# Blocks 2 and 3 of a fused attention and feed-forward kernel: h for both blocks first, y by seven products, preparation jobs and opening reordered

## The chip, the cores and the metric

The kernel runs on one core of a Trainium2 chip. The metric is the time of one execution in microseconds (us), as the device reports it; three executions are shown, and their median counts.

## What is computed

Chunked attention (chunks of 32 queries, 8 memory keys, 16 keys to the left, 8 to the right), then two feed-forward layers over 3072 tokens (model width 512, inner width 2048), all in float32:

```python
scores = scale * np.matmul(q_c, k_full.transpose(0, 1, 3, 2))
a = np.exp(scores - np.max(scores, axis=-1, keepdims=True))
a = a / (np.sum(a, axis=-1, keepdims=True) + 1e-09)
out[:, :, c_start:c_end] = np.matmul(a, v_full)
...
h = x @ w_in                                              # layer 1
g = np.maximum(h, 0.0) + np.log1p(np.exp(-np.abs(h)))
y = g @ w_out
...
h = y @ w_in2                                             # layer 2
g = h - np.tanh(h)
out = g @ w_out2
```

## The kernel before

**Numbers in halves.** A float32 operand is kept as a high part (a float32r copy, made by ScalarE, ACT) and a low part (the rest, a subtraction on VectorE, DVE). `mm3` makes one product of two such operands by three matmuls on TensorE (PE): high x high, high x low, low x high. The weights come as 64-bit numbers, whose words are put together by integer work on ACT and DVE (`split_w` in the opening, `job_w` later).

**Blocks.** Tokens are worked in six blocks of 512, an attention unit being 128 tokens (24 units). Layer 1 gives y from h through g: `ff_h` makes one of 16 rows of h (12 matmuls with 512 columns), softplus gives g, `split_g` its halves `gh`, `gl`, and `ff_y1` adds that row's part to the four banks of y (12 matmuls). Block 0 runs in the opening, whose order of work stands written out by hand as tokens (`OPENING`); blocks 1, 2 and 3 alternate h and y row by row (the loop over `j` with `PLAIN`), with h in two PSUM banks (`ps_h`) and y in the four `ps_y`. Blocks 4 and 5 make all of h first (`steps`, 32 of them, h in six banks in turn) and then y for both blocks at once by seven products instead of eight (`y_phase`), as in Strassen's scheme: 7 products x 8 rows x 2 halves of the width x 3 matmuls. Layer 2 (three blocks of 1024 tokens, `PHASES`) uses seven products for h and for y. `y_steps` makes the operands of these products: per product and row a cast `gh` on ACT, a subtraction `gl` on DVE, in some steps a sum on DVE. The first three (`AHEAD`) are made ahead, and the pool `g` has three buffers for each, so the operand for row k+3 waits until PE is through with row k.

**Order of the work.** The order on every engine is the program's (a manual schedule). Behind every 12 matmuls of h, and every 12 of y, the program calls `tick()`, whose counter places everything else: attention units 8 to 23 one after the other, each starting six ticks behind the last (`ATT_STEP`, `ATT_ORDER`), and the preparation jobs at the ticks in `JOBS`: eight `job_w1` (sums of layer 1's output weights for the seven products), sixteen `job_w` (layer 2's weights: loaded at once, worked on from the fourth tick on, written back to HBM as seven operands), six `job_x` (layer 2's seven inputs for a block of 1024 tokens, made from y of layer 1). In a unit, tick 0 issues on PE the attention output of the unit before (`v_mm`) and this unit's scores (`s_mm`), and on DVE the maximum and a subtraction; tick 1 the exponential on ACT; tick 2 the sum and division on DVE; tick 4 the transposes on PE (`t_mm`). Softplus and the exponential need different tables on ACT, so a table load (`ACT_TABLE_LOAD`) stands in front of each change. Transfers are all issued from SyncE's queue (SP), in the program's order. `Ring` loads the weights of the seven products ahead, through five slots of 1 MB.

**Places that the change touches.** `OPENING` (tokens: Z zero products that PE runs to fill time, S scores, T transposes, V attention output, H and Y rows of layer 1, `l` the low part of a weight, K the storing of layer 1's weights for later; `ON_POOL` puts the named low parts on GpSimd, POOL), `VIA_DRAM` (units 20 to 22 come early in the order and go through HBM), `job_w`, `job_x`, `Ring`, `h_phase`, `y_phase`, `tick` and the main loops.

Of the kernel before, what the change touches and what calls it, by code (L numbers as in the profile page):

```python
# [22 lines left out]
P = 128  # L23
# [11 lines left out]
N = 512  # L35
# [27 lines left out]
ON_POOL = ('li0', 'l15')  # L63
# [12 lines left out]
PLAIN = NB - 2  # L76
# [4 lines left out]
GSLOT = (8, 9, 10, 11, 12, 13, 14, 7)  # L81
JOBS = (
    (1, 15, 24, 43, 53, 76, 85, 94),
    (5, 14, 23, 33, 66, 75, 84, 92, 95, 99, 102, 106, 109, 113, 117, 152),
    (42, 54, 159, 169, 214, 224),
)
SECOND = (95, 102, 109, 117)
PHASES = ((1, NT - 1),) + tuple((2, b) for b in range(NT))
# [8 lines left out]
def attention_ffn_ffn(  # L97
# [38 lines left out]
    x1d = dpool.tile([P, KT, 2, N], F32, name="x1d")  # L136
# [927 lines left out]
```

## Time and profile before

| what | value |
|---|---|
| median of three executions | 1057.54 us (1057.13 to 1058.17) |
| the profiled execution | 1057.51 us |
| its span, first to last instruction | 1055.4 us |
| mean granted clock of TensorE, share of full | 0.997 |
| busy in the span: PE, DVE, ACT, POOL | 1044.2, 727.6, 567.1, 7.8 us |
| moved by DMA | 303.19 MB, mean 287 GB/s |

The span is what the rows of the trace cover; the profiled execution is 2.1 us longer, for what lies around it. A busy time is the sum of an engine's instructions. Matmuls are pipelined and their ends are modelled, so PE's pace is read from the starts of its rows rather than from its busy time. In the lists of instructions each row has a start, a duration, engine, line and operation, and in brackets the engine's idle time before it with the work that ended it.

### The profile page before, as it was taken

Reading aid. Unit: us, or ns where it says so; the run is one execution under the profiler, and the core shown is the slowest. Engines: PE = TensorE matmul, PEld = TensorE weight load, DVE = VectorE, ACT = ScalarE, POOL = GpSimd, SP = SyncE. Lnnn points to the kernel's source line nnn. Section 1 sums busy time; section 2 is a strip of 40 time slices with the busy share of each in tenths; the row PEclk is TensorE's granted clock in tenths of the full one; section 3 lists DMA queues with packets and bytes.
Section 4 is the critical chain, followed back from the end, with each engine's and each line's share of the span. In section 5 each row is a group of like instructions: output and inputs, shape, how many; then the busy total and the mean of one; then the engine's idle time right before and its main releaser. Section 6 shows DMA issues by size and latency. Waiting matters only on the chain.

```text
span 1055.4 us, 18458 instructions
## 1 busy us (share of the span) xinstructions
PE 1044.2 (99%) x7368; PEld 857.4 (81%) x7370; DVE 727.6 (69%) x1129; ACT 567.1 (54%) x904; POOL 7.8 (1%) x14
## 2 busy tenths in 40 slices
PE   7999999999999999999999999999999999999998
PEld 5787888888888888888888888888888888888886
DVE  6998445845755657487677687777487877446876
ACT  6996454645656455354454555544455554344553
POOL 2000000000000000000000000000000000000000
PEclk8999999999999999999999999999999999999999
DMA  9989945857777986999987999978799788656651
GB/s 377 407 327 358 337 171 186 301 187 236 263 248 248 312 307 195 341 361 352 325 326 281 359 371 347 341 294 320 272 363 347 293 321 305 224 170 213 243 202 61
DMA packets 101269, 303.19 MB, mean 287 GB/s; under 512 B 8000, under 2 KB 55104, under 8 KB 83520
## 3 DMA queue, kind: packets, MB, share of 16 engines
q1 hardware_dynamic: 101184, 302.02, 79.5%
q8 instruction: 58, 0.95, 0.4%
q14 instruction: 27, 0.22, 0.1%
HBM read 211.29 MB, written 90.70 MB: 286 GB/s over the span
## 4 chain that ended last, share of the span: by engine, by line
PE 97%; DVE 1%; ACT 1%; DMA 0%; issue 0%; ACTq 0%
PE ps_y L387 47%; PE ps_h L387 32%; PE ps_b L387 13%; PE ps_a L361 2%; PE ps_a L280 1%; PE ps_a L332 1%; PE ps_h L880 1%; DMA qk<-in_qk 0%; PE ps_yy L361 0%; PE ps_h L399 0%; DVE gl L427 0%; DVE t L307 0%; DVE x L327 0%; ACT o L170 0%; PE ps_a L268 0%
## 5 line engine op out<-in xcount | busy, mean ns | idle before, releaser
L387 PE MATMUL ps_h<-x,w 128*128 128x512 f32 x900 | 215.3, 390 | 0.1
L704 ACT CAST gh<-w 128x512 fp32r<-128x512 f32 x224 | 139.0, 622 | 140.3 <-DVE gl L645 120.2
L645 DVE TENSOR_TENSOR gl<-w,gh 128x512 fp32r<-128x512 f32 x236 | 163.0, 691 | 71.4 <-ACT gh L704 64.9
L387 PEld LDWEIGHTS ps_h<-x,w 128*128 128x128 f32 x900 | 168.6, 188 | 35.4 <-ACT t L410 0.2
L387 PE MATMUL ps_y<-gh,w 128*128 128x512 f32 x512 | 172.9, 399 | 0.0
L387 PEld LDWEIGHTS ps_y<-gh,w 128*128 128x128 f32 x512 | 96.1, 188 | 21.3
L387 PE MATMUL ps_y<-gh,x 128*128 128x512 f32 x352 | 109.4, 389 | 0.0
L387 PE MATMUL ps_y<-gl,w 128*128 128x512 f32 x256 | 99.7, 390 | 0.0
L387 PE MATMUL ps_y<-w,x 128*128 128x512 f32 x402 | 94.5, 389 | 0.0
L387 PEld LDWEIGHTS ps_y<-w,x 128*128 128x128 f32 x402 | 75.5, 188 | 15.7
L427 DVE TENSOR_TENSOR gl<-t,gh 128x512 fp32r<-128x512 f32 x64 | 45.5, 713 | 55.8 <-ACT gh L422 55.6
L668 ACT ACTIVATE tanh<-sum 128x512 f32<-128x512 f32 x72 | 45.5, 632 | 60.0 <-DVE sum L641 59.8
L387 PEld LDWEIGHTS ps_y<-gh,x 128*128 128x128 f32 x352 | 66.1, 188 | 13.7
L410 ACT ACTIVATE t<-ps_h 128x512 f32<-128x512 f32 x64 | 38.1, 598 | 69.4 <-PE ps_h L387 65.8
L387 PE MATMUL ps_b<-gh,x 128*128 128x512 f32 x176 | 68.5, 389 | 0.0
L387 PE MATMUL ps_h<-gh,x 128*128 128x512 f32 x176 | 68.5, 389 | 0.0
L387 PE MATMUL ps_y<-gl,x 128*128 128x512 f32 x176 | 68.5, 389 | 0.0
L448 ACT CAST o<-c 128x1024 fp32r<-128x1024 f32 (+1 forms) x32 | 31.0, 969 | 69.6 <-DVE c L493 41.1
L645 DVE TENSOR_TENSOR w<-w 128x512 f32<-128x512 f32 x88 | 60.5, 688 | 6.8 <-ACT w L410 5.8
L387 PEld LDWEIGHTS ps_y<-gl,w 128*128 128x128 f32 x256 | 48.2, 188 | 9.0
L387 PE MATMUL ps_y<-x,w 128*128 128x512 f32 x240 | 55.2, 389 | 0.0
L387 PE MATMUL ps_b<-w,x 128*128 128x512 f32 x216 | 54.8, 389 | 0.0
(160 smaller groups left out, 1611.6 us busy)
## 6 DMA issues: line engine op xcount, KB each, us to landing
x<-wod SPq DMA_DIRECT2D x44, 1024.0 KB, 4.7
w<-x2d SPq DMA_DIRECT2D x21, 1024.0 KB, 6.8
x<-wid SPq DMA_DIRECT2D x21, 1024.0 KB, 6.1
wod<-o SPq DMA_DIRECT2D x32, 512.0 KB, 6.1
qk<-in_qk SPq DMA_DIRECT2D x21, 768.0 KB, 6.5
x2d<-o SPq DMA_DIRECT2D x30, 512.0 KB, 7.2
x<-wid SPq DMA_DIRECT2D x18, 768.0 KB, 6.8
ring<-wod SPq DMA_DIRECT2D x12, 1024.0 KB, 5.3
```

Of the source, the lines that this page charges most:

```text
L280: nc.tensor.matmul(out=ps[cc, j, KEYS * p : KEYS * (p + 1)], lhsT=a["q"][r, p, cc], rhs=a["k"][r, c, p, :], start=True, stop=True,)
L332: nc.tensor.transpose(ps[:, p * P : (p + 1) * P], a["sm"][:, p * P : (p + 1) * P], ident)
L361: nc.tensor.matmul(out=ps[h : h + 64, p % 2, 2 * P + t0 : 2 * P + t0 + CHUNK], lhsT=v, rhs=pT, start=True, stop=True,)
L387: nc.tensor.matmul(out=ps, lhsT=a, rhs=b, start=first and i == 0, stop=last and i == 2, skip_group_check=on,)
L410: nc.scalar.activation(out=out, in_=x, func=AF.Softplus)
L427: eng.tensor_tensor(out=gl, in0=t, in1=gh.bitcast(F32), op=ALU.subtract)
L448: nc.scalar.copy(out=hi, in_=src)
L645: nc.vector.tensor_tensor(out=out, in0=x, in1=y, op=ALU.subtract)
L668: nc.scalar.activation(out=t, in_=h, func=AF.Tanh)
L704: nc.scalar.copy(out=gh, in_=src)
L880: nc.tensor.matmul(out=ps_h[1], lhsT=zeros[:, :P], rhs=zeros, start=True, stop=True)
```

## The change

1. **Blocks 2 and 3** are worked as blocks 4 and 5 are: 32 steps of h (block 2 with rows 0 to 15, then block 3 with rows 15 to 0), then y of both by seven products (`y_phase(0)`), with y in the four banks `ps_y` and weights from a ring in slots `w0` to `w4`. Only block 1 still alternates. `PHASES` gets a first phase, the loads of layer 1's weights get ticks of their own (`T1_LOADS`), and the ring for the later phases is made apart.
2. **Attention** goes in plain order, at ticks written out (`ATT_AT`); units 20 to 22 no longer go through HBM. Units 10, 11, 21 and 22 (`LATE_ACT`) get the form of softmax that the opening uses for some units: eight small exponentials on ACT that also add up, in place of one wide one with a subtraction and a sum on DVE. Units with four ticks have their transposes at tick 3 in place of 4. Units 20 to 23 now lie beside `y_phase(0)`.
3. **Jobs** get other ticks. Nine of the sixteen `job_w` (`BY_ACT`) put their words together with two more passes on ACT and two fewer on DVE. Two of the sums become one. The jobs that work between ticks 105 and 121 split in two pieces, with tiles of the pool `g` (`split_halves`).
4. **Opening**: zero products in more and smaller groups (8, 4, 1, 2, 3, 7, 2 in place of 7, 8, 11), some tokens in another order, one low part (`li0`) on DVE in place of POOL, `K` tokens elsewhere.

```diff
-ATT_STEP = 6
-ATT_ORDER = (8, 9, 10, 11, 20, 12, 13, 14, 15, 21, 16, 17, 18, 19, 22, 23)
-VIA_DRAM = (20, 21, 22)
+ATT_AT = (0, 6, 14, 20, 28, 33, 38, 42, 46, 50, 54, 59, 64, 68, 74, 86, 92)
...
-Z7 S0 mx0 qa1 qb1 ex0 Z8 S1 ml0 qa2 qb2 T0 mx1 qa3 S2 pT0 qb3 ex1 S3 mx2 mx3 ex2 V0 ml1 ex3 ml2 T1
-yi0 ml3 T2 xh0 pT1 xl0 T3 pT2 si0 V1 yo0 pT3 xh1 V3 so0 hi0 y1 li0 V2 xh3 xl1 xh2 xl3 y2 s1 xl2 Z11
-H0 h1 s2 ho0 S4 l1 h2 y3 H1 l2 K1 c10 s3 y4 H2 c30 lo0 h3 c40 c11 l3 Y0 c31 y5 s4 H3 c41 h4 s5 c12
+Z8 S0 mx0 qa1 qb1 ex0 Z4 S1 qa2 ml0 qb2 qa3 Z1 T0 mx1 S2 pT0 qb3 ex1 S3 mx2 mx3 ex2 Z2 V0 ml1 ex3
+ml2 T1 yi0 ml3 Z3 T2 xh0 pT1 xl0 T3 pT2 si0 V1 yo0 pT3 V3 xh1 so0 hi0 y1 xl1 V2 xh3 li0 xl3 xh2 s1
+y2 xl2 Z7 H0 h1 s2 S4 ho0 l1 h2 y3 Z2 H1 l2 K1 c10 s3 y4 H2 c30 lo0 h3 c40 c11 l3 Y0 c31 y5 s4 H3
...
-ON_POOL = ('li0', 'l15')
+ON_POOL = ('l15',)
...
 JOBS = (
-    (1, 15, 24, 43, 53, 76, 85, 94),
-    (5, 14, 23, 33, 66, 75, 84, 92, 95, 99, 102, 106, 109, 113, 117, 152),
-    (42, 54, 159, 169, 214, 224),
+    (3, 8, 4, 11, 18, 22, 25, 28, ),
+    (8, 15, 27, 37, 43, 49, 55, 89, 96, 99, 102, 105, 108, 111, 131, 148, ),
+    (86, 94, 156, 169, 206, 220, ),
 )
-SECOND = (95, 102, 109, 117)
-PHASES = ((1, NT - 1),) + tuple((2, b) for b in range(NT))
+SECOND = (89, 96, 102, 108, )
+BY_ACT = (8, 15, 27, 55, 99, 108, 111, 131, 148, )
+T1_LOADS = {9: 0, 13: 1, 17: 2, 21: 3, 25: 4, 29: 5, 33: 6, 38: 7, 54: 0}
+LATE_ACT = (10, 11, 21, 22, )
+T2_H = (105, 121)
+PHASES = ((1, 1), (1, 2)) + tuple((2, b) for b in range(NT))
...
+        if by_act:
+            x = pool.tile([P, 4 * HALF, 2], U16, name=name, bufs=1)
+            nc.scalar.mul(x[:, :, 1].bitcast(F16), hi.bitcast(F32), SIGN_ONLY)
+            nc.scalar.activation(
+                out=x[:, :, 0], in_=lo, func=AF.Identity, scale=LOW_SCALE, bias=low_bias
+            )
+            nc.scalar.mul(hi.bitcast(F32), hi.bitcast(F32), EXP_BIAS)
+            yield
+            c = x.rearrange("p n two -> p (n two)").bitcast(U32)
             nc.vector.scalar_tensor_tensor(
-                out=c, in0=of, scalar=k, in1=c, op0=op, op1=ALU.bitwise_or
+                out=c, in0=hi, scalar=3, in1=c, op0=ALU.logical_shift_left, op1=ALU.bitwise_or
             )
+        else:
...
-        if r == 4 and u is not None:
+        t = min(4, ATT_AT[i + 1] - ATT_AT[i] - 1) if u is not None else -1
+        if r == t:
             t_mm(u, ps_a[:, 0, :])
...
-            soft[u] = softmax(u)
+            soft[u] = softmax(u, u in LATE_ACT)
...
-        for j in range(1, PLAIN):
-            x = x_tile(j)
-            for f in range(NF):
...
+        x = x_tile(1)
+        for f in range(NF):
+            ps = ff_h(f, ps_h[slot % 2], x)
+            tick(chain1((1, 1, f), ps, nc.scalar))
...
+        steps = [(0, f) for f in range(NF)] + [(1, f) for f in reversed(range(NF))]
+        prep = y_steps(prepared, t2)
+        ring = Ring((0,), ())
+        for n, (t, f) in enumerate(steps):
+            if t and f == NP - 1:
+                t2.extend(t2_tiles())
+            h_step(n, n == len(steps) - 1, t, f, x_tile(2 + t), t and f < NP and t2)
...
+            if t and f % 2 == 0 and f < 2 * T_RING:
+                s = T1_RING[T_RING - 1 - f // 2]
+                defer(lambda s=s: ring.add(wpool.tile([P, 2048], F32R, name=f"w{s}")))
+        y_phase(0, prep, prepared)
```

Three places show what moves. The rows are instructions in their order on one engine, line, operation, tile written and tile read; a number behind a name tells one use of a tile from the next. Lines differ between the two kernels, since the file grew.

**ACT, unit 21's exponentials.** Before, a unit's exponential stands between the rows of a block that alternates h and y, with a table load for it (L321) and one for the next softplus (L410):

```order
L321 ACT_TABLE_LOAD
L321 ACTIVATE sm_3601<-sm_3601 128x512
L535 CAST o_3627<-w15_3333 128x512
L535 CAST o_3648<-w15_3333 128x512
L410 ACT_TABLE_LOAD
L410 ACTIVATE t_3650<-ps_h1_82 128x512
L422 CAST gh_3652<-t_3650 128x512
```

With the change, unit 21's stand among the casts `gh` of `y_phase(0)`:

```order
L748 CAST gh_4070<-w10_2782 128x512
L677 COPY t_4074<-ps_y0_670 128x512
L322 ACT_TABLE_LOAD
L322 ACTIVATE sm_4048,st_4047<-ps_a_86,st_4047 128x64 x8
L748 CAST gh_4094<-w11_2803 128x512
L677 COPY t_4099<-ps_y2_672 128x512
L748 CAST gh_4107<-w12_2826 128x512
```

A load and eight exponentials thus stand between two casts that PE's products wait for. Unit 22's eight stand likewise, without a load.

**DVE and PE, unit 20's softmax at the start of the seven products.** Before, the operands of the first seven products (blocks 4 and 5) had no unit beside them: on DVE the `gl` followed one another. With the change, DVE's order there is this (w8 is waited for from the last softplus, which stands on ACT behind unit 20's exponential and two table loads):

```order
L686 TENSOR_TENSOR gl_3894<-w10_2782,gh_3893 128x512
L686 TENSOR_TENSOR w8_2620<-w8_2620 128x512
L686 TENSOR_TENSOR w5_3572<-w8_2620 128x512
L686 TENSOR_TENSOR gl_3913<-w11_2803,gh_3912 128x512
L686 TENSOR_TENSOR gl_3923<-w12_2826,gh_3922 128x512
L330 TENSOR_REDUCE st_3868<-sm_3869 128x8
L331 TENSOR_SCALAR st_3868<-st_3868 128x8
L332 RECIPROCAL st_3868<-st_3868 128x8
L333 TENSOR_TENSOR sm_3869<-sm_3869,st_3868 128x2x4x64
```

And on PE the transposes that read this `sm` stand behind the fourth row of products (`gh_3912`):

```order
L384 MATMUL ps_y2_672<-gl_3913,w1_3586 128x512
L384 MATMUL ps_y2_672<-gh_3912,w1_3586 128x512
L338 MATMUL ps_a_86<-ident_134,sm_3869 128x128 x4
L384 MATMUL ps_y0_670<-gh_3922,w2_3702 128x512
```

So PE's fifth row of products now stands behind a softmax.

**ACT, the weight job of tick 131 (tick 117 before).** Before, the one job that came into the seven products of blocks 4 and 5 had its first instruction behind the last cast:

```order
L704 CAST gh_6044<-w12_4932 128x512
L704 CAST gh_6055<-w13_4977 128x512
L704 CAST gh_6066<-w14_5018 128x512
L704 CAST gh_6078<-w7_5061 128x512
L468 ACTIVATE c2_6088<-w15_5998 128x1024
L726 COPY o_6115<-ps_h0_81 128x512
```

With the change, one job's three passes stand in the middle of them (and another's behind the last):

```order
L748 CAST gh_5811<-w6_5569 128x512
L487 ACTIVATE c2_5815<-w15_5719 128x1024
L488 ACTIVATE c2_5815<-w15_5719,low_bias_135 128x1024
L491 ACTIVATE w15_5719<-w15_5719 128x1024
L748 CAST gh_5827<-w6_5569 128x512
```

Between two casts there are now three passes of 1024 elements.

## Rows read from the trace of the kernel before

**Rows 1.** The page: PE's busy time, and the chain that ended last by engine.

```profile
PE 1044.2 (99%) x7368; PEld 857.4 (81%) x7370; DVE 727.6 (69%) x1129; ACT 567.1 (54%) x904; POOL 7.8 (1%) x14
...
PE 97%; DVE 1%; ACT 1%; DMA 0%; issue 0%; ACTq 0%
```

**Rows 2.** Waits of PE: engine, line waited for, us in total, times, longest.

```profile
PE ps_yy L332 <- DVE x L327: 1.6, 2, 1.2
PE ps_a L332 <- DVE sm L327: 1.2, 1, 1.2
```

**Rows 3.** PE in order of time, block 0: start, us, line, operation, count.

```profile
40.98 2.88 PE L387 MATMUL ps_h<-x,w 128*128 128x512 f32 x12
43.70 0.39 PE L387 MATMUL ps_y<-gh,w 128*128 128x512 f32 x1
```

**Rows 4.** All engines in order of time, the opening.

```profile
22.12 3.64 PE L361 MATMUL ps_yy<-x,w 64*64 64x32 f32 x128
...
26.10 3.08 PE L880 MATMUL ps_h<-gl 128*128 128x512 bf16 x10 [0.33 <-issue]
...
28.48 0.68 DVE L377 TENSOR_TENSOR x<-ps_yy,x 128x512 fp32r<-128x512 f32 x1
...
28.83 3.10 PE L399 MATMUL ps_h<-x,w 128*128 128x512 f32 x12
...
30.06 1.23 DVE L178 SCALAR_TENSOR_TENSOR o<-o,c 128x1024 uint32<-128x1024 uint32 x1 [0.89 <-ACT c L174]
```

**Rows 5.** Busy by stretch; the column behind POOL is PE's granted clock.

```profile
24.00:26.00 2.00, 1.76 (x68) 1.76 (x66) 1.71 (x3) 0.90 (x3) 1.01 (x1) 0.50 1.05 417
```

**Rows 6.** All engines in order of time, seven products of blocks 4 and 5.

```profile
587.63 0.39 PE L387 MATMUL ps_b<-gh,x 128*128 128x512 f32 x1
587.83 0.62 ACT L704 CAST gh<-w 128x512 fp32r<-128x512 f32 x1 [0.74 <-PE ps_h L387]
...
588.48 0.69 DVE L645 TENSOR_TENSOR gl<-w,gh 128x512 fp32r<-128x512 f32 x1 [0.23 <-ACT gh L704]
...
588.99 0.39 PE L387 MATMUL ps_b<-gh,x 128*128 128x512 f32 x1
```

**Rows 7.** Groups by line and shape: busy us, mean ns of one, idle before.

```profile
L645 DVE TENSOR_TENSOR w<-w 128x512 f32<-128x512 f32 x88 | 60.5, 688 | 6.8 <-ACT w L410 5.8
...
L327 DVE TENSOR_TENSOR sm<-sm,st 128x512 f32<-128x512 f32 x20 | 13.8, 692 | 0.7
...
L321 ACT ACT_TABLE_LOAD x17 | 21.8, 1283 | 0.3
...
L468 ACT ACTIVATE c<-w 128x1024 f32<-128x1024 f32 x12 | 13.6, 1133 | 5.1 <-DVE o L452 5.1
L410 ACT ACTIVATE w<-ps_y 128x512 f32<-128x512 f32 x20 | 11.7, 594 | 4.0 <-PE ps_y L387 4.0
...
L174 ACT ACTIVATE c<-w,low_bias 128x1024 uint16<-128x1024 uint32 x4 | 5.9, 1469 | 0.0
L173 ACT ACTIVATE c<-w 128x1024 f16<-128x1024 f32 x4 | 5.5, 1384 | 0.0
```

**Rows 8.** ACT in order of time, unit 5: table load, first and last exponential of eight.

```profile
84.33 1.28 ACT L316 ACT_TABLE_LOAD   x1
85.63 0.31 ACT L316 ACTIVATE sm<-ps_a,st 128x64 f32<-128x64 f32 x1
...
87.86 0.24 ACT L316 ACTIVATION_READ_ACCUMULATOR sm<-ps_a,st 128x1 f32 x1
```

**Rows 9.** DVE, then POOL, in order of time, 95 to 106.

```profile
98.08 2.35 DVE L427 TENSOR_TENSOR gl<-t,gh 128x512 fp32r<-128x512 f32 x1
...
97.48 2.40 POOL L198 TENSOR_TENSOR w<-o,w 128x1024 fp32r<-128x1024 f32 x1 [72.48 <-ACT w L196]
```

**Rows 10.** Busy by stretch, h of blocks 4 and 5; last two columns DMA share, GB/s.

```profile
448.55:474.90 26.36, 26.36 (x118) 21.83 (x117) 22.51 (x32) 13.53 (x19) 0.00 (x0) 1.00 1.01 362
474.93:501.30 26.37, 26.37 (x118) 21.81 (x118) 18.67 (x26) 12.75 (x19) 0.00 (x0) 1.00 1.02 352
```

More of the change, by code (lines that the diff above doesn't have):

```diff
@@ L1 @@
+from bisect import bisect_right
 from contextlib import ExitStack
@@ L75 @@
 SHARED = (7, 15)
-PLAIN = NB - 2
 T_LAG = 3
@@ L444, in out1, with split_halves @@
             defer(nc.sync.dma_start, y1d[j // 2][e % 2][:, j % 2, e // 2], o, more=1)
+    def split_halves(src, dst):
+        for s in range(2):
+            ts = []
+            for i in (0, 2):
+                t = gpool.tile([P, 2, HALF], F32R, name="gl" if s else "gh")
+                if s:
+                    nc.vector.tensor_tensor(
+                        out=t, in0=src[:, i : i + 2], in1=his[i // 2].bitcast(F32), op=ALU.subtract
+                    )
+                else:
+                    nc.scalar.copy(out=t, in_=src[:, i : i + 2])
+                ts.append(t)
+            if s:
+                for i, t in enumerate(ts):
+                    defer(put, t, ((0, 2, dst(1, 2 * i)),))
+            else:
+                his = ts
+                yield
+                for i, t in enumerate(ts):
+                    put(t, ((0, 2, dst(0, 2 * i)),))
     def split_to(src, dst, shape):
@@ L485, in job_w @@
         yield
-        yield from split_to(w, lambda s: ((0, 4, place(s, 2, 4)),), [4, HALF])
+        if T2_H[0] <= now[0] < T2_H[1]:
+            yield from split_halves(w, lambda s, i: place(s, 2 + i, 2))
+        else:
+            yield from split_to(w, lambda s: ((0, 4, place(s, 2, 4)),), [4, HALF])
     def sums(w):
@@ L516, in job_w1, with job_x @@
         yield from split_to(c, lambda s: ((0, 4, wod[0][:, 2:6, p, s]),), [4, HALF])
-    def job_x(b, e, second=False):
-        raw = wpool.tile([P, 2, 2, N], F32, name="w6" if second else "w15")
+    def job_x(b, e, slot):
+        raw = wpool.tile([P, 2, 2, N], F32, name=f"w{slot}")
         nc.sync.dma_start(out=raw, in_=y1d[b][e])
@@ L741, in y_phase @@
         for i, q in enumerate(PRODUCTS):
-            ps = [banks[(2 * b + d) % 4][i % 2] for d in range(2)]
+            ps = [(banks[2 * (b - 1) + d & 3] if b else ps_y[2 * d : 2 * d + 2])[i % 2] for d in range(2)]
             for p in range(NP):
@@ L800, in tick @@
                 run(soft.pop(u))
-        if r == 1 and before in VIA_DRAM:
-            run(soft.pop(("x", before)))
+        if k in T1_LOADS:
+            t_load(T1_LOADS[k], T1_SLOT[T1_LOADS[k]])
         active.extend(job() for job in plan.get(k, ()))
@@ L951, in act_g, with h_step @@
                 minus(g, g, g0)
-        for n, (t, f) in enumerate(steps):
-            ps = ps_h[(slot + n) % 2] if n < 4 else (*ps_y, *ps_h)[(n - 4) % 6]
+            if t2:
+                minus(t2[f // 4][:, f % 4], g2[f][:, 3], g)
+        def h_step(n, last, t, f, x, t2=None):
+            ps = ps_h[n % 2] if n < 4 else (*ps_y, *ps_h)[(n - 4) % 6]
             weights["i", f] = w1t["i", f]
-            ff_h(f, ps, xs[t])
+            ff_h(f, ps, x)
             if f < NP and not t:
```

207 lines of the change are left out of this document (107 added, 100 removed).

## Prediction

> **What bounds the kernel now.** I read the page's busy times and chain first, then PE's waits, then PE in order of time. PE is busy 99% of the span and carries 97% of the chain [rows 1]. Its waits for others are a few single ones of 1.2 us at most, all for a softmax in front of transposes [rows 2]; the one on `ps_a` lies near 105 us and is the last, so behind it nothing is waited for. PE's pace comes from starts: twelve products of 512 columns take 43.70 - 40.98 = 2.72 us, 0.2267 each [rows 3]. So a matmul saved is 0.2267 us saved, as long as ACT, DVE and the transfers stay hidden. The question is where the new order uncovers them.
>
> **What is saved.** Blocks 2 and 3 cost 2 x 32 x 12 = 768 matmuls before; now 32 x 12 for h and 7 x 8 x 2 x 3 = 336 for y, 720 in all. 48 x 0.2267 = **10.9 us off PE**. Attention issues the same matmuls as before. The four transfers through HBM for units 20 to 22 go; they lay beside PE's work and give nothing.
>
> **The opening.** Between the last attention output and row 0 of h stand eleven zero products, now seven, and two more follow before row 1. Ten took 28.83 - 26.10 = 2.73 us, 0.27 each [rows 4], so row 0 could start 1.1 us earlier. It has the reserve: its ninth product needs the low part that DVE ends at 28.48 + 0.68 = 29.16, and comes at 28.83 + 8 x 0.2267 = 30.64. `li0`, now on DVE, takes 0.69 of that reserve of 1.48 (and is regained where DVE idles 0.89 us for ACT [rows 4]), the shift 1.1: 0.3 short. Two zeros before row 1 give 0.5 back, so about 0.3 stays. Work ahead of it may come sooner as well: the clock stood at 0.50, the 1.2 GHz level, while PE made the last attention outputs [rows 5], 3.64 us for two units [rows 4]; at 2.4 GHz they could take half. Bounds: 0.7 lost (`li0` uncovered) to 2.9 gained (1.1 + 1.8). I take **0.7 gained**, near the counted end, since DVE's chain, not PE, ends the opening.
>
> **The reserve of the seven products.** Before, hardly anything stood between the operands of this phase; now attention and a weight job do. A row of products lasts 6 x 0.2267 = 1.36. After PE ends row k (587.63), the cast for row k+3 starts at 587.83, takes 0.62, and the low part is ready at 588.48 + 0.69 = 589.17, that is 1.54 later [rows 6]. Row k+3 begins 2.72 after the end of row k and its second matmul, which reads the low part, 2.95 after: reserve 1.41 us. Whatever goes between two casts and lasts longer stops PE. Three places do.
>
> (1) *Unit 20, the phase's start.* Count from the end of its scores. PE has twelve h products left (to 2.72), then four rows (to 8.16), then the transposes. ACT makes three casts (to 1.8), a table load 1.28, the exponential 0.6, a load 1.28, the last softplus 0.59: 5.6 [rows 6, 7]. DVE waits for that softplus, then two differences (0.69 each), two low parts, and the four operations of the softmax (0.69 + 0.17 + 0.20 + 0.69): 10.2 [rows 7]. The transposes start there in place of 8.16: **2.1 us**, handover included.
>
> (2) *Units 21 and 22.* Their eight exponentials last 87.86 + 0.24 - 85.63 = 2.47 us, with the load before them 3.77 [rows 8]. Unit 21: the cast ends 0.82 after the row, a copy of 0.59 follows, then 3.77, then cast and low part: 6.5, against a need at 4.31 (one row later than 2.95): 2.2. Its division on DVE, some 1.1 us in front of a low part, costs 0.4 more. Unit 22 has no load: 0.82 + 2.47 + 0.62 + 0.72 = 4.63, so 0.3. Together **2.9 us**.
>
> (3) *The weight job of tick 131.* Three passes, 1.38 + 1.47 + 1.13 = 3.99 [rows 7], stand between two casts: low part at 0.82 + 3.99 + 0.62 + 0.72 = 6.15 against 4.31: 1.85. Three ticks later its low part and sums, 1,800 elements in four operations, take some 2.5 us on DVE (0.69 per 512 [rows 7]): 1.54 + 2.5 + 0.69 = 4.73 against 4.31, 0.4. Together **2.3 us**. The job of tick 148 falls behind the last cast, where the job before the change stood too, and costs nothing.
>
> Each place could cost nothing only if its work ran ahead of its turn, which the program's order excludes; from above the reserve is none, 1.41 more for each late operand (one, three and two: 3.5, 7.1 and 5.1). I keep to the reserve, which is read from the same kind of phase.
>
> On (1) and (2) a rule is to be weighed. The row of a load shows 1283 ns and the activation starts 0.02 us behind it (84.33 + 1.28, then 85.63) [rows 8]. The Trainium skill ("ScalarE: Activation LUTs", What ACT_TABLE_LOAD costs) gives 1283 ns and a drain of some 1380 ns besides for every change of set. By the rows the sum is as above; by the page each of the three loads here would cost 1.38 more, 4.1 us in all, and eat most of what is left of the gain.
>
> **What I cost at nothing.** The h steps of blocks 2 to 5 write six PSUM banks in turn, so ACT may be 5 x 2.72 = 13.6 us late; bursts there are 3.99 or 3.77. In block 1 a bank comes back after three times 2.72, 8.2 us. The first four steps after the phase have only two banks: the fourth waits for a softplus behind a job's cast, by my count with 0.1 us to spare; 0 to 1.5, taken as 0. The slow low part of 2.35 us beside POOL's subtraction, and the wait behind it [rows 9, 2], stay: `l15` is still on POOL. Weights for the added products are 14 loads of 1 MB, five ahead, 27 us of cover. SP's other new waits (a raw load into a slot of `g2` at tick 94, first-layer loads behind ring slots) find their slots free some two ticks before. Past the phase of blocks 4 and 5 the order is the old one, four ticks earlier; jobs there stay in the h phases.
>
> **Sum.** Against the profiled execution, 1057.51, which is within 0.03 of the median: 1057.51 - 10.88 - 0.7 + 2.1 + 2.9 + 2.3 = **1053.2 us**. About 0.2% (2.1 us) is what a measurement of this kernel can tell from no change.
>
> **Rivals.**
>
> *A. The operands run further ahead than I think* (17%). Then (2) and (3) vanish and (1) stays, since transposes wait for their softmax in any case: 1053.2 - 5.2 = 1048.0. For it: attention's own matmuls in these ticks lengthen PE's rows and give ACT time. Against it: three buffers, and a cast that starts 0.20 behind a row's end [rows 6].
>
> *B. The transfers of the jobs fall behind, slower* (7%). Between ticks 92 and 111, beside h of blocks 4 and 5, the changed program issues 27.3 MB (before, in its densest twenty ticks, 21) in 20 x 2.72 = 54.4 us, 500 GB/s. With the engines full the queue moved 352 to 362 GB/s in that stretch [rows 10], so 27.3 MB take 76 us and the queue ends 22 late. Jobs give a load four ticks, 10.9 us; the other 11 fall on ACT, with the passes of two or three jobs of 3.99 behind them. Once ACT is more than 13.6 us late PE stops: 11 + 8 - 13.6 = 5.4 to 9.4, so 1059 to 1063, I take 1061. Against it: jobs that wait issue their next transfers later, and the full engines of [rows 10] stopped PE nowhere [rows 2].
>
> *C. The opening does not do what it says* (15%). Four zeros in place of eight behind the first scores may leave the clock at 1.2 GHz until row 0, whose twelve products would take twice 2.72; with the 0.7 not gained that is 3.4: 1056.6. Or the first steps after the phase cost their 1.5 and smaller bursts the like: 1056. No change in both. For it: the clock did fall in the opening before [rows 5]. Against it: the seven zeros directly before row 0 stay.
>
> *D. A change of tables costs about twice its row* (3%). Three loads more uncovered by 1.28 each: 1057.0, no change. Against it: 0.02 us between load and activation [rows 8]. That is the skill's rule above, with which its own row agrees in the load and not in the drain.
>
> My forecast has 58%, with 1051.5 to 1055.8 as its own range, most of it over 0.2% faster (54 of 58).
>
> **Numbers.** Faster: 54 + 17 + 3 of C = 0.74; same: 4 of the forecast + 12 of C + 3 of D = 0.19; slower 0.07 (B). The range 1047.5 to 1058.0 takes in A, C and D and leaves out B and the tails of A and of the opening's gain.
>
> **What would show it.** PE has 48 fewer matmuls of 512 columns, and row 0 starts near 28 us. PE's waits gain rows for `gh` or `gl` in the seven products of blocks 2 and 3: transposes of unit 20 waiting 1 to 2 us for the softmax, a stop of 2 us behind eight exponentials, and one of 1.8 in the phase of blocks 4 and 5 behind a job's three passes. All else stays at 0.2267 a matmul. I am wrong if those three places run at pace (A), if PE waits in the h steps of blocks 4 and 5 for ACT that waits for a raw load (B), or if row 0 starts after 28.8 (C).

## The result and the profile after

The changed kernel takes **1066.69 us** (median of four, 1066.05 to 1071.15) against 1057.34 of the kernel before: ratio 1.0098, 95% interval 1.0069 to 1.0127. It is slower by 9.4 us where the prediction said 4.3 faster. The profiled execution is the longest of the four (1071.15, span 1069.4), so its stops are some 4 us longer than usual. Medians, ratios and intervals here and below are of fast executions alone: one of c2's ten (1871.85 us) and one of the 21 of the kernel before beside it were slow.

The page of the changed kernel, against [rows 1] (the second row is the DMA queue: packets, MB, share of its sixteen engines): PE does less work, 1039.3 us, in a longer span, and the chain now runs through DMA and ACT.

```profile
PE 1039.3 (97%) x7323; PEld 847.1 (79%) x7323; DVE 743.6 (70%) x1149; ACT 607.7 (57%) x1011; POOL 6.2 (1%) x13
...
q1 hardware_dynamic: 100816, 318.80, 82.3%
...
PE 84%; DVE 6%; DMA 5%; ACT 3%; issue 2%; ACTq 0%; DVEq 0%; SPq 0%
```

The stages, from the start of each one's first product to that of the next (profiled executions; c5 is the last kernel below):

| stage, us | before | changed | c5 |
|---|---|---|---|
| start of blocks 2 and 3 | 229.5 | 228.8 | 229.4 |
| blocks 2 and 3 | 201.7 | 200.8 | 199.3 |
| h of blocks 4 and 5 | 87.04 | 98.86 | 87.06 |
| y of blocks 4 and 5 | 76.16 | 78.41 | 76.16 |
| layer 2 | 461.0 | 462.5 | 462.4 |

Blocks 2 and 3 give 0.9 us in place of 5.9. The largest loss, 11.8 us, is in h of blocks 4 and 5, whose matmuls the change doesn't touch (9.1 us in the profiles of e3 and e4 below, which have the same jobs there: 96.1 us). PE's waits, against [rows 2] (engine, line waited for, us in total, times, longest; L407 is the softplus, L748 the cast of the operands, L333 the division):

```profile
PE ps_h L384 <- ACT w L407: 5.0, 2, 3.7
PE ps_a L338 <- DVE sm L333: 4.1, 3, 2.2
PE ps_y L384 <- ACT w L407: 4.0, 2, 3.3
PE ps_y L384 <- ACT gh L748: 2.0, 2, 1.4
...
PE ps_y L384 <- issue: 1.7, 1, 1.7
```

The first and the third row, 9.0 us, are waits for a softplus, that is for a PSUM bank that is free again once ACT has read it: ACT is late. Why ACT is late is in the waits of the other engines in this phase (425 to 530 us; L466 and L470 the high and low parts of a weight job in the o buffers, L453 and L449 in the g buffers):

```profile
DVE gl L449 <- DMA wod<-gl: 9.4, 4, 4.9
...
ACT gh L453 <- DMA wod<-gh: 6.0, 2, 5.5
...
ACT o L466 <- DMA y1d<-o: 4.9, 1, 4.9
```

ACT and DVE stand for buffers that earlier stores still hold. The first stop in order of time:

```profile
434.13 0.60 ACT L407 ACTIVATE w<-ps_h 128x512 f32<-128x512 f32 x1
...
440.25 0.83 ACT L466 CAST o<-w 128x768 fp32r<-128x768 f32 x1 [4.88 <-DMA y1d<-o]
440.99 1.08 ACT L407 ACTIVATE w<-ps_h 128x512 f32<-128x512 f32 x2
...
441.63 1.58 PE L384 MATMUL ps_h<-x,w 128*128 128x512 f32 x3 [3.74 <-ACT w L407]
```

A job's cast waits 4.88 us for a store of y (`y1d<-o`) to land, two softplus stand behind it in ACT's order, and PE, which has only two banks here, waits 3.74. The transfers in these stretches (the column behind POOL is PE's clock, then DMA share and GB/s) are full:

```profile
430.00:470.00 40.00, 36.26 (x153) 29.54 (x152) 22.22 (x32) 16.94 (x27) 0.00 (x0) 0.96 1.00 348
470.00:510.00 40.00, 36.05 (x158) 29.11 (x157) 26.37 (x39) 22.43 (x32) 0.00 (x0) 1.00 1.00 351
```

How much was too much is in the rows of the whole stage, in the kernel before, the changed one, and c5:

```profile
431.23:518.27 87.04, 87.04 (x386) 72.07 (x384) 59.39 (x84) 40.15 (x58) 0.00 (x0) 1.00 0.95 334
429.57:528.43 98.86, 89.88 (x386) 72.87 (x384) 59.37 (x86) 53.09 (x79) 0.00 (x0) 0.98 1.00 347
428.69:515.75 87.06, 87.06 (x385) 72.07 (x384) 54.93 (x78) 50.57 (x74) 0.00 (x0) 1.00 0.99 346
```

Time times rate gives 29.1, 34.3 and 30.1 MB. At the 346 to 347 GB/s of full engines 34.3 MB take the 98.9 us that the stage lasted; 30.1 MB take 87, which is PE's own pace. Most of what came in are outputs of block 0's two x2 jobs (`job_x`), some 6 MB which the kernel before has stored ahead of this stage (its jobs start at ticks 42 and 54, those of the changed kernel at 86 and 94).

So rival B is what happened, if by a shorter way than it said: not loads late for their job, but stores late to free the buffer of the next. The experiments had to tell whether bytes, passes or buffers are the cause.

### The profile page after: what moved, and what is told of

Read it like the earlier page. It is cut to its first block, busy times and chain, and to the rows that moved or that the text cites. A ratio compares the mean times of both kernels' runs of the same rounds, so it can differ in the third digit from the quotient of the medians.

```text
span 1069.4 us, 18606 instructions
## 1 busy us (share of the span) xinstructions
PE 1039.3 (97%) x7323; PEld 847.1 (79%) x7323; DVE 743.6 (70%) x1149; ACT 607.7 (57%) x1011; POOL 6.2 (1%) x13
## 4 chain that ended last, share of the span: by engine, by line
PE 84%; DVE 6%; DMA 5%; ACT 3%; issue 2%; ACTq 0%; DVEq 0%; SPq 0%
PE ps_y L384 45%; PE ps_h L384 22%; PE ps_b L384 12%; PE ps_a L367 2%; PE ps_a L286 1%; DMA w<-w1id 1%; DMA x2d<-o 1%; DVE gl L686 1%; DMA y1d<-o 1%; PE ps_a L338 1%; DMA wod<-gh 1%; DVE w L686 1%; DMA wid<-o 1%; DMA wod<-gl 1%; DVE o L195 0%
## 5 line engine op out<-in xcount | busy, mean ns | idle before, releaser
L686 DVE TENSOR_TENSOR gl<-w,gh 128x512 fp32r<-128x512 f32 x298 | 204.8, 690 | 95.4 <-ACT gh L748 88.3
L748 ACT CAST gh<-w 128x512 fp32r<-128x512 f32 x280 | 173.5, 624 | 171.8 <-DVE gl L686 126.6
L384 PE MATMUL ps_h<-x,w 128*128 128x512 f32 x660 | 160.0, 395 | 5.1 <-ACT w L407 5.0
L384 PE MATMUL ps_y<-gh,w 128*128 128x512 f32 x480 | 158.9, 399 | 1.4 <-ACT gh L748 1.4
L384 PEld LDWEIGHTS ps_h<-x,w 128*128 128x128 f32 x660 | 124.4, 190 | 32.6 <-ACT w L407 5.9
L384 PE MATMUL ps_y<-x,w 128*128 128x512 f32 x480 | 113.8, 393 | 5.6 <-ACT w L407 4.0
L384 PEld LDWEIGHTS ps_y<-x,w 128*128 128x128 f32 x480 | 89.1, 188 | 25.6 <-ACT w L407 4.8
L384 PEld LDWEIGHTS ps_y<-gh,w 128*128 128x128 f32 x480 | 90.8, 189 | 21.5 <-ACT gh L748 1.8
L686 DVE TENSOR_TENSOR w<-w 128x512 f32<-128x512 f32 x104 | 71.6, 688 | 17.8 <-ACT w L407 16.5
L686 DVE TENSOR_TENSOR w<-w,w 128x512 f32<-128x512 f32 x80 | 54.9, 686 | 0.0
L682 DVE TENSOR_TENSOR sum<-ps_y,kept 128x512 f32<-128x512 f32 x36 | 24.9, 691 | 42.4 <-PE ps_y L384 35.2
```

The lines of the kernel that those rows point to most:

```text
L384: nc.tensor.matmul(out=ps, lhsT=a, rhs=b, start=first and i == 0, stop=last and i == 2, skip_group_check=on,)
L682: nc.vector.tensor_tensor(out=h, in0=ps, in1=t, op=ALU.add)
L686: nc.vector.tensor_tensor(out=out, in0=x, in1=y, op=ALU.subtract)
L748: nc.scalar.copy(out=gh, in_=src)
```

## The experiments

**Which part of the jobs stops PE.** Theory: bytes. Rivals: the passes on ACT and DVE; the g buffers; the two banks (no run takes these away by themselves). Behind each median below stand its ratio to the kernel before and the 95% interval. A stop's length in the text is counted between starts, some 0.2 us more than the idle time in a row's brackets.

*f1: six weight jobs without their passes.* In `job_w`:

```diff
-        if by_act:
+        if 96 <= now[0] - LEAD - 1 <= 111:
+            c = pool.tile([P, 4 * HALF], U32, name=name, bufs=1)
+            yield
+            nc.vector.tensor_scalar(out=c, in0=hi, scalar1=3, scalar2=None, op0=ALU.logical_shift_left)
+        elif by_act:
```

> The changed kernel with the weight jobs of ticks 96 to 111 stripped of the passes that rebuild the 32-bit weight (one scaling on ACT or three passes there, two or one combining passes on DVE; one shift on DVE stays), so that the weights of the second layer that these six jobs make are not the reference's. Loads, sums, casts, low parts and stores stay: the same bytes. Each job loses 1.1 or 4.0 us on ACT and 1.2 to 2.4 on DVE. Theory 1 (transfers are late): h of blocks 4 and 5 stays within 3 us of the changed kernel's 96 to 99 us. Rival (the passes on ACT are late): it falls below 91.

1066.22 us (1.0074, 1.0046 to 1.0101). h of blocks 4 and 5 took 96.8 us. With 1.1 to 4.0 us less on ACT per job, ACT and DVE just wait longer for the same stores:

```profile
DVE gl L449 <- DMA wod<-gl: 18.7, 5, 8.8
...
ACT gh L453 <- DMA wod<-gh: 10.6, 4, 6.9
```

The passes of these six jobs are not what makes the stage long: with them it took 96.1 us in e3 and e4. They share in where PE stops: in the changed kernel the last two stops, at 505 and 515 us, stand behind three passes of 3.6 us together, which start late because DVE waits for `wod<-gl`; in f1 the second of these stops is gone.

*f3: no half tiles* (`T2_H = (0, 0)`, all through the o buffers).

> The changed kernel with the second part of its weight jobs in the phase always kept in the o buffers, as in the kernel before, instead of half tiles in the gh and gl buffers. Theory 1 (the bytes are the limit, whichever buffer they wait in): h of blocks 4 and 5 within 3 us of 96 to 99. Rival (the g buffers, each held by a slow store, are the bottleneck): it falls below 92, and the stops near 500 and 512 us go.

1068.91 us (1.0111, 1.0085 to 1.0138), h of blocks 4 and 5 98.2. The g buffers are not the cause either.

*f2: more bytes in the kernel before.* In its `put`:

```diff
             nc.sync.dma_start(out=place, in_=t[:, at : at + n].bitcast(F32))
+            if n == 4 and 98 <= now[0] <= 130:
+                nc.sync.dma_start(out=place, in_=t[:, at : at + n].bitcast(F32))
```

> The kernel before, with the two 512 KB stores of the second part of each weight job between ticks 98 and 130 issued twice, to the same place: seven jobs, some 7 to 8 MB more to move, no pass more on ACT or DVE. A count of what is issued per tick against 350 GB/s leaves 5.5 MB undone at tick 111 and 8 at tick 119 in place of 1.4 to 2.0 (8.0 at tick 111 in the changed kernel). Theory 1 (transfers beyond the rate stop PE by way of the buffers): h of blocks 4 and 5 grows from 87.0 us to 92 to 102, with ACT and DVE waiting for wod<-o. Rival (the kernel before has the slack, and what stops the changed one is its own order of passes or its split buffers): within 1 us of 87.0.

1107.28 us (1.0467, 1.0447 to 1.0488), h of blocks 4 and 5 129.7 us, far more than expected, and not for the reason expected. Two rows, the queue's waits of 430 to 562 us and a stretch of it:

```profile
SPq L459 <- DMA wod<-o: 66.8, 13, 8.7
```

```profile
470.00:510.00 40.00, 25.34 (x86) 19.40 (x84) 17.59 (x25) 10.55 (x15) 0.00 (x0) 0.83 0.82 263
```

The second store to a place waits on SP for the first, 13 times, and everything behind it in the queue waits too; the engines moved 263 GB/s, not 350. The run shows that a held store stops PE by way of the buffers, not that the rate does. So the bytes were added in another way:

*g1: the same bytes to places of their own, in the kernel before.*

```diff
             nc.sync.dma_start(out=place, in_=t[:, at : at + n].bitcast(F32))
+            if n == 4 and 98 <= now[0] <= 130:
+                spare = dpool.tile([P, 4, HALF], F32, name=f"spare{len(spares)}")
+                spares.append(spare)
+                nc.sync.dma_start(out=spare, in_=t[:, at : at + n].bitcast(F32))
```

> The kernel before with the two 512 KB stores of the second part of each weight job between ticks 98 and 130 issued a second time, now each to a place of its own that nothing reads, so that no store waits for another: the same 7 to 8 MB more as in the run with doubled stores, whose stops came from SP standing for the first store of each pair (66.8 us) while the engines moved only 263 GB/s. Nothing more on ACT or DVE. Theory 1 (bytes beyond the rate hold the buffers, and through them ACT, DVE and PE): transfers run at 340 to 360 GB/s with a share near 1, and h of blocks 4 and 5 grows from 87.0 to 91 to 100 us. Rival (the order of the passes in the changed kernel is needed for the stops): within 1 us of 87.0, with ACT and DVE waiting for stores but PE not.

1067.45 us (1.0078, 1.0055 to 1.0102): 9.5 us slower from transfers alone, 8.9 MB of them (310.9 MB in the queue for 302.0). h of blocks 4 and 5 grew from 87.04 to 95.8, y to 78.4. (The profiled execution, 1071.21, has 3.0 us of a late opening besides; see e4.) The stretch shows full engines, and the waits the same chain as in the changed kernel:

```profile
470.00:510.00 40.00, 36.38 (x152) 29.21 (x151) 26.12 (x39) 15.32 (x22) 0.00 (x0) 0.96 1.04 388
```

```profile
ACT o L449 <- DMA wod<-o: 12.0, 2, 7.1
DVE o L453 <- DMA spare<-o: 10.3, 5, 5.1
...
ACT o L449 <- DMA y1d<-o: 8.0, 1, 8.0
```

*g2: fewer bytes in the changed kernel's stage.* The other halves are stored between ticks 66 and 83 instead, from other data.

```diff
-            nc.sync.dma_start(out=place, in_=t[:, at : at + n].bitcast(F32))
+            part = P // 2 if 102 <= now[0] <= 124 else P
+            nc.sync.dma_start(out=place[:part], in_=t[:part, at : at + n].bitcast(F32))
```

> The changed kernel with the stores of the six weight jobs of ticks 96 to 111 cut to half the partitions (5 MB fewer between ticks 102 and 124; every load, cast, pass and wait stays), the other halves filled with other data in the seven products of blocks 2 and 3, where transfers have room; the weights of the second layer are thus not the reference's. Theory 1 (bytes): h of blocks 4 and 5 falls from 96 to 99 to 87 to 92 us, and what stays are the stops before tick 102 (the one near 437 us, about 3 us and some half clock). Rival (the number of stores and passes, not their bytes): it stays above 94.

1064.63 us (1.0052, 1.0029 to 1.0075). h of blocks 4 and 5 took 93.0 us: all its stops behind tick 102 are gone, the one that begins near 439 us (3.4 us, and half clock behind it) stays. Its stretches:

```profile
428.00:468.00 40.00, 36.72 (x155) 29.86 (x155) 23.90 (x34) 17.32 (x28) 0.00 (x0) 0.96 1.01 368
468.00:508.00 40.00, 40.00 (x177) 32.85 (x176) 30.07 (x44) 25.87 (x36) 0.00 (x0) 1.00 0.91 299
```

This is 1 us above the range I gave and on the side of the bytes: with the share at 0.91 PE runs at pace through the same passes and the same number of stores. g1 and g2 together settle it for the stops behind tick 102. The first stop they leave as it is. It seems to need the two banks as well as a late store, for in c5 ACT waits longer at about the same place and PE runs on (below). (g2's h of blocks 2 and 3 is 2.5 us longer than the changed kernel's, though the other data are issued only behind it: a longer stop at 240, with half clock behind it.)

**Where the bytes can go.** *e1: the jobs spread*, W and X being the lists of `JOBS`:

```diff
-W 8, 15, 27, 37, 43, 49, 55, 89, 96, 99, 102, 105, 108, 111, 131, 148   X 86, 94, 156, 169, 206, 220
+W 8, 15, 27, 32, 36, 41, 45, 50, 55, 95, 99, 103, 107, 111, 131, 148    X 76, 86, 156, 169, 206, 220
```

> The changed kernel with the weight jobs and the two x2 jobs of block 0 started earlier: x2 jobs at ticks 76 and 86 in place of 86 and 94; weight jobs at 32, 36, 41, 45, 50, 55 in place of 37, 43, 49, 55 and 89, and at 95, 99, 103, 107, 111 in place of 96 to 111. Ticks 92 to 111 then issue some 19 MB in place of 27.3. Theory 1 (the transfers of the jobs fall behind; ACT and DVE stand behind stores, PE behind ACT): h of blocks 4 and 5 falls from 98.9 us to 87 to 89, the stops of 3.9, 3.5 and 1.4 us there go, the waits for wod<-gh and wod<-gl fall below 2 us each; the total falls by 8 to 11 us less what the x2 job in the seven products of blocks 2 and 3 costs there (0 to 2). Theory 2 (the passes of the jobs on ACT and DVE are what is late, or the two banks of the first steps): five jobs instead of six still stand in the phase, so h of blocks 4 and 5 stays above 94 us and the third step still stops for 3 to 4 us.

1076.54 us (1.0184, 1.0150 to 1.0218). h of blocks 4 and 5 fell to 87.04, as expected, but h of blocks 2 and 3 grew by 7.5 us and their y by 9.2: the total is worse. The first half of the theory held; the 0 to 2 us put on the x2 job did not. That job now stands among the seven products and takes the g buffers of their operands (ACT waits 2.6 us for a store of x2 before a cast). In h of blocks 2 and 3 attention's operands come later: PE stops 3.7 us at 240 (2.4 in the changed kernel), where DVE waits 6.5 us for a job's store, and 2.4 us at 338, where a job's cast on ACT waits 5.3 us for DVE.

*e2: the job of tick 131 at 117.*

> The changed kernel with the weight job of tick 131 (in y of blocks 4 and 5) at tick 117 (in h). Theory of the prediction: y of blocks 4 and 5 falls from 78.4 us to 76.2, its pace, and h of these blocks stays as it is or grows by under 1 us, as ticks 117 to 125 are light: total 2 us less. Rival (the stops in y come from operands that are late for another reason): y stays at 78.

1073.83 us (1.0138, 1.0111 to 1.0164). A miss: h of blocks 4 and 5 grew to 102.2 and the backlog ran into y (79.3, stops of 2.6 and 1.4 us at its start); some 4 us of its profile are a late opening (e4, below). The place that looked light, ticks 117 to 125, was still working off what the ticks before had issued: the stage moved 35.5 MB at 347 GB/s.

*e3: units 21 and 22 with the wide softmax* (`LATE_ACT = (10, 11)`).

> The changed kernel with the softmax of units 21 and 22 in the wide form (one subtraction and one sum on DVE, one exponential on ACT) in place of eight exponentials. Theory of the prediction (the eight exponentials stand between two casts): the stops at 356.8 and 358.6 us (1.6 and 0.5) fall to some 0.3 to 0.8, since the table load of 1.28 stays; with them goes the half clock of 360.1 to 363.5, if it follows from the stop, 1.6 us more: 2.5 to 3.5 us less. Rival (DVE is what is late there): DVE gets two operations of 0.69 more per unit, the stops stay or grow, the total is the same or up to 2 us more.

1065.46 us (1.0064, 1.0049 to 1.0079), 1.2 below the changed kernel's median; the intervals overlap, so the total does not show the 2.5 to 3.5 us. In the profile y of blocks 2 and 3 fell from 90.8 to 87.7 us; both stops are gone, and a wait of 0.5 us for DVE is left. For the stops the theory of the prediction holds. The half clock is gone too, but that proves nothing: e4, f3 and g2 have the stops without it, and take 89.3 us there.

*e4: the old opening in the changed kernel; c4: the new opening in the kernel before.*

> The changed kernel with the opening of the kernel before (its order, eleven zero products at one place, li0 on POOL). The prediction and the trace of the changed kernel: the start of blocks 2 and 3 comes 0.7 us later (229.5 in place of 228.8) and the total grows by 0.7. Rival (the shift of the opening is taken back by the waits behind it, by transfers that have their own time): the total is the same within 0.3 us.

> The kernel before with nothing changed but the opening (the new order, its zeros, li0 on DVE). By the prediction and the changed kernel's early profiles: 0.7 us less, 1056.7. If the new opening has two outcomes: early runs 0.7 less, late ones 3 to 4 more, the median between 1056.5 and 1060.

e4: 1067.13 us (1.0093, 1.0066 to 1.0121), blocks 2 and 3 start at 230.2 in place of 228.8; the totals, 0.4 apart, can't be told from each other. c4: 1057.02 against 1057.55 (0.9993, 0.9984 to 1.0002), no difference that can be told; its profiled execution took 1060.46. The opening has two outcomes. In eight of eleven profiles of the new one row 0 starts at 24.4 to 25.1 us and waits for its operand's low part:

```profile
24.43 2.18 PE L396 MATMUL ps_h<-x,w 128*128 128x512 f32 x8
...
28.42 1.83 PE L396 MATMUL ps_h<-x,w 128*128 128x512 f32 x4 [1.81 <-DVE x L380]
```

In three (e2, c1, c4) it starts at 31.1 to 31.5. There PE stops for 2.3 to 3.9 us after 24 of the 128 matmuls of the last attention outputs, each time at this place and with nothing awaited that the profile shows; from e2:

```profile
21.79 0.55 PE L367 MATMUL ps_yy<-x,w 64*64 64x32 f32 x24 [0.66 <-ACT x L350]
26.00 3.00 PE L367 MATMUL ps_yy<-x,w 64*64 64x32 f32 x104 [3.66 <-issue]
...
31.54 3.49 PE L396 MATMUL ps_h<-x,w 128*128 128x512 f32 x12
```

The 104 matmuls behind the stop, at half clock, take 3.0 us (in the changed kernel's profile all 128 take 2.07), and the end of the opening comes some 4 us later. The old opening has this outcome too: in g1, one of its five profiles, PE stops 3.5 us after 27 of the same 128 matmuls, and row 0 starts at 31.45 in place of 28.8 to 29.7. So the late start does not come with the new order alone. What PE waits for is not in the rows, but the packed traces show a companion. The page lists an instruction queue, q8, which moves 58 transfers of 16 KB in every run. Every stop of PE of over 0.6 us for which nothing is awaited, 23 in the sixteen profiles, ends 2.2 to 2.6 us after the start of one of them. In the four late openings that transfer starts at 23.2 to 23.5 us, in the twelve others at 18.5 to 19.5. This speaks for PE waiting for its own instructions; no run tests it, and why the transfer comes late stays open.

**A version that levels the transfers.** I counted what the program issues per tick against 350 GB/s. Before, 1.4 to 2.0 MB are undone at ticks 111 to 119; in the changed kernel 8.0 at tick 111, an estimated 23 us of transfers; in c1 at most 3.4 at any tick. This is what the program would be behind if nothing waited, not a length of the queue: in the traces the transfers issued and not yet landed are 2.9 MB on average in this stage of the changed kernel and 2.8 in c5, since engines that wait issue later. *c1*, with W and X:

```diff
-W 8, 15, 27, 37, 43, 49, 55, 89, 96, 99, 102, 105, 108, 111, 131, 148   X 86, 94, 156, 169, 206, 220
+W 8, 15, 24, 32, 38, 43, 49, 55, 97, 102, 105, 108, 111, 114, 148, 161  X 76 (half pace, o buffers), 92, 155, 168, 206, 220
-LATE_ACT = (10, 11, 21, 22, )
+LATE_ACT = (10, 11, )
```

> The changed kernel with its transfers levelled, by a count of what is issued per tick against 350 GB/s: at most 3.4 MB are undone at any tick in place of 8.0. Weight jobs at 8, 15, 24, 32, 38, 43, 49, 55, then 97, 102, 105, 108, 111, 114, then 148 and 161 (was 131, in y of blocks 4 and 5); x2 jobs of block 0 at 76, at half the pace and through the o buffers, and 92; of block 1 at 155 and 168; units 21 and 22 with the wide softmax. Theory 1: h of blocks 4 and 5 falls to 87 to 90, y of blocks 4 and 5 to 76.2 (no job there), h of blocks 2 and 3 to 108 to 110 with the stop near 240 under 1 us, y of blocks 2 and 3 88 to 91: total 1050 to 1056, faster than the kernel before. Rival (the whole stretch up to tick 180 is full, and what is taken from one stage comes back in the next): the sum stays at 1060 or more.

1059.54 us (1.0020, 1.0004 to 1.0036), above the 1050 to 1056 of the theory. h and y of blocks 4 and 5 took 87.04 and 76.16 us, their pace, and y of blocks 2 and 3 87.6. But a job's cast now stood on ACT in front of the copy that attention waits for (PE 2.65 us at 230, half clock behind it), and the opening was late.

*c2 and c3* move three jobs of c1 (weight jobs from 24 to 22 and 161 to 160, an x2 job from 168 to 166; 38 stays); c3 has the old opening as well.

> c1 with four jobs moved: the weight job of tick 24 at 22, 37's stays at 38, 161 at 160, and the second x2 job of block 1 at 166 in place of 168. In c1's profile the cast of the job of tick 24 stood on ACT between a unit's transposes and the copy of them, and PE waited 2.65 us at 230 us with the clock at half for 6.8 us behind it. Theory 1 (levelled transfers, and no long job cast in front of the copy that attention waits for): the stop at 230 us and the half clock go, 4 to 6 us less in that stage; the stops of 0.5 us at the start of y of the second layer's block 0 go as well (1.0): 1053 to 1056 us, faster than the kernel before. Rival (the stop moves to another unit's copy, or the start of the program varies by more than that): 1058 or more.

> c2 with the opening of the kernel before. Row 0 of h came at 24.4 to 25.0 us in six profiles of the changed opening and at 31.3 and 31.5 in two (c1 and the job at 117), with the clock at half for 6.8 us before it; with the old opening at 28.8 to 29.7 in three. If the new opening has two outcomes, c3 is 0.7 to 1.4 us slower than the early runs of c2, some 2.5 to 3 faster than the late ones, and its runs lie closer together; the medians within 1.5 us of each other. If the late start was an accident of two runs, c3 is 0.7 to 1.4 us slower than c2 throughout.

1060.76 (1.0032, 1.0016 to 1.0049) and 1064.14 (1.0055, 1.0043 to 1.0067). Misses: the stop near 230 us stayed (2.5), one of 2.2 for transposes came at 224, and the jobs at 160 and 166 stopped PE at 648, 3.0 us in c2 and 2.5 in c3. The profiled openings were an early one and the old one, and the medians are 3.4 apart instead of 1.5 at most; I don't know what the other 1.9 is. (The two profiled executions, 1064.04 and 1064.93, are only 0.9 apart.)

*c5* takes the early jobs back to the changed kernel's places (W 8, 15, 27, 37, 43, 49, 55, 89, then 97 to 114 as in c1, 148, 161); the rest is c1's.

> c1 with the weight jobs ahead of tick 90 as the changed kernel has them (8, 15, 27, 37, 43, 49, 55, 89) and six more at 97 to 114; the rest as in c1 (148 and 161, x2 jobs at 76 at half pace, 92, 155, 168, the wide softmax). c1 and c2 lost 5 to 6 us around 220 to 231 us, where jobs of ticks 22 to 32 stand beside the attention units, and 1.8 near 280; the changed kernel with the wide softmax lost 2.1 at 240 alone. The count against 350 GB/s leaves 3.2 MB undone at tick 111 (c1 1.2, the changed kernel 8.0). Theory 1 (both rates count: bytes in h of blocks 4 and 5, passes in front of attention's copies): start of blocks 2 and 3 at 229 us, h of blocks 2 and 3 109 to 110, y 87.7, h of blocks 4 and 5 87 to 88.5, y 76.2, the second layer 462.5: 1053 to 1056 us. Rival (3.2 MB undone are enough to stop PE there): h of blocks 4 and 5 90 to 94 and a total of 1057 or more.

**1055.42 us**, ratio 0.9977 (0.9962 to 0.9991): faster than both kernels, than the one before by 0.2%. Page, the same phase, and ACT's longest wait for a store in it:

```profile
PE 1034.2 (98%) x7323; PEld 845.6 (80%) x7323; DVE 746.1 (71%) x1150; ACT 604.2 (57%) x980; POOL 6.2 (1%) x13
...
PE 89%; DVE 6%; ACT 2%; DMA 2%; issue 1%; ACTq 0%; SPq 0%; DVEq 0%
```

```profile
456.00:496.00 40.00, 40.00 (x178) 33.14 (x177) 27.11 (x38) 25.29 (x36) 0.00 (x0) 1.00 1.02 371
```

```profile
442.00 0.62 ACT L570 CAST o<-w 128x512 fp32r<-128x512 f32 x1 [7.04 <-DMA x2d<-o]
```

The DMA engines are as full as in the changed kernel, 371 GB/s here, and PE has no stop in this phase. ACT still waits 7.0 us for a store once, longer than the 4.88 that stopped PE in the changed kernel; but here two softplus instead of one ran ahead of the wait, so both banks were free. Full engines do not stop PE as long as the bytes of a stage fit into its time. The cause is not gone everywhere: y of blocks 2 and 3 took 89.7 us, not the 87.7 expected, 1.9 of it at 426, where a job's cast on ACT waits 4.8 us for a store in front of a cast of the products. The same 318.8 MB at other ticks, with what goes along with the ticks (which jobs take the three passes, the buffers of an x2 job), and the wide softmax of two units are together worth 11 us; the runs do not part them.

## Why the prediction was wrong

**The step that failed** stands in "What I cost at nothing": "ACT may be 5 x 2.72 = 13.6 us late; bursts there are 3.99 or 3.77". The bursts were read from ACT's passes; the lateness came from stores. The same paragraph gave the fourth step behind the seven products "0.1 us to spare; 0 to 1.5, taken as 0": it stopped 3.9 us (441.63), with a job's cast in front of its softplus that waited 4.88 us for a store. I had the right count in rival B (27.3 MB in 54.4 us against 352 to 362 GB/s, 22 us late) and gave it 7%, because "jobs that wait issue their next transfers later" and because the full engines of [rows 10] stopped PE nowhere. Both were weak. [Rows 10] are a stretch in which, by my count, 1.4 to 2.0 MB were undone, and the whole stage moved 29.1 MB there; a share of 1.01 says nothing about how much is still to come. And the jobs do wait, but ACT and DVE wait with them, in their one order, and the softplus behind. B added 7.8 us in my sum; h of blocks 4 and 5 lost 11.8 in the profiled execution, 9.1 in those of e3 and e4.

Term by term:

- *48 matmuls, -10.9 us.* Right: in c5, where little stops it, PE's busy time is 10.0 below that of before. But the queue now moves 318.8 MB in place of 302.0, 14.7 of them in the 14 loads for the added products. Most of these fall into y of blocks 2 and 3, where the queue still has room (238 GB/s, share 0.66); the price came in h of blocks 4 and 5, into which the x2 jobs went. It was in no term of the sum: "five ahead, 27 us of cover" asks whether one load is in time, not whether a stage's bytes fit into its time.
- *Opening, -0.7.* Right in size where it goes early (228.8 for 229.5, though e4 makes it 1.4 and c4 can't show it). The way was another than forecast: row 0 starts at 24.4, not "near 28" (the 128 matmuls ahead of it take 2.07 us instead of 3.64), then PE waits 1.8 us for its low part, and row 1 starts at 31.8 for 32.7. Three profiles of eleven are some 4 us late, near rival C's 3.4, but not by its mechanism: PE stops first and the clock falls during that stop, and one profile of the old opening does the same.
- *(1) Unit 20, 2.1.* The transposes waited 0.5 us. PE had stopped 1.8 us a few products earlier, in the last step of h, and that gave DVE its time: in c3, the one kernel of this order without that stop, a low part and the transposes waited 0.5 and 0.95 us. So the forecast was nearer than the 0.5 says. The stop (1.5 to 2.9 us in the others) is one of the 23 named under e4: nothing is awaited, and it ends 2.3 to 2.4 us after a transfer of the instruction queue starts.
- *(2) Units 21 and 22, 2.9.* The mechanism is right. Table load, eight exponentials, cast, then PE:

```profile
354.25 1.28 ACT L322 ACT_TABLE_LOAD   x1
355.55 0.32 ACT L322 ACTIVATE sm<-ps_a,st 128x64 f32<-128x64 f32 x1
...
357.88 0.65 ACT L748 CAST gh<-w 128x512 fp32r<-128x512 f32 x1
...
358.58 0.51 PE L384 MATMUL ps_y<-gh,w 128*128 128x512 f32 x1 [1.40 <-ACT gh L748]
```

  Unit 21 cost 1.6 + 0.5 (forecast 2.2 + 0.4), unit 22 nothing (0.3); the half clock behind the stop was in no term. It costs 1.5 us (90.8 for 89.3) in three profiles with these stops and is absent in four. The activation starts 0.02 us behind the load, as in [rows 8]: the drain of some 1380 ns in the Trainium skill ("ScalarE: Activation LUTs", What ACT_TABLE_LOAD costs) is not seen here either, and rival D falls.
- *(3) The job of tick 131, 2.3.* Measured 2.25 (78.41 for 76.16), and back to 76.16 without it in c1 and c5.
- *Not foreseen at all:* 2.4 us at 240, where transposes wait for a division that stands behind DVE's copies of y, and these wait 5.2 us for a store of a job; 1.5 us in layer 2, most of it at the start of its first y.

```profile
DVE o L438 <- DMA wid<-o: 5.2, 1, 5.2
...
PE ps_a L338 <- DVE sm L333: 2.2, 1, 2.2
```

The three places where I expected PE to wait for operands were all real, and their sum (some 6 us with the half clock, against 7.3) is a quarter of the 25.6 that the profile lost against the two savings.

## What to carry to other kernels

When a change trades matmuls for loads, or moves jobs that load and store, put the transfers in the sum: the bytes of each stage against its time and the rate that the trace shows (here 347 GB/s and PE's 87 us, so 30 MB), with what is left over carried from stage to stage. A DMA share near 1 tells that the rate is reached, not how far behind the program is; the sign to look for is compute engines waiting for a buffer that a store holds. Work that is placed in the order of an engine which others depend on should have its buffers free before its turn, not just its operands.

## What the runs showed that I had not expected

- A stop of PE can cost more than its length. After the stops near 358 and 441 us the granted clock stood at half (the 1.2 GHz level) while PE was already working again; after the one of 3.5 us at 504.9 it did not (last row):

```profile
360.10:363.50 3.40, 3.40 (x10) 2.63 (x9) 3.13 (x7) 0.62 (x1) 0.00 (x0) 0.54 0.36 100
...
442.00:445.40 3.40, 3.40 (x10) 2.59 (x10) 0.00 (x0) 0.06 (x1) 0.00 (x0) 0.54 0.98 398
...
505.00:508.40 3.40, 3.40 (x15) 2.82 (x16) 2.35 (x3) 2.73 (x5) 0.00 (x0) 1.00 1.00 368
```

  Ten matmuls took 3.40 us where the pace is 2.27. The same stops of unit 21 (1.6 and 0.5 us) are followed by half clock in the changed kernel, e2 and f1, and not in e1, e4, f3 and g2; what decides it is not shown.
- A second store to the same place is held back on the issuing queue until the first has landed (66.8 us in 13 waits in f2), with all that stands behind it.
- A small move of a job can do harm: moved by two ticks (24 to 22, c2), it kept its stop of 2.5 us, and another of 2.2 came some 6 us ahead of it.
